# A new order of loads, masks and first outputs in the start-up of a fused attention and gated feed-forward kernel

## The chip, the cores and the metric

The kernel runs on one core of a Trainium2 chip. The metric is the device time of one execution in microseconds (us). The profile covers a "span" that is about 2.1 us shorter than that time, and all moments below are counted from the start of the span. PE is the matrix engine, PEld its weight loads, DVE the vector engine, ACT the scalar engine, POOL the engine that issues the casting loads. In these traces each engine works through its instructions in the order in which the program gives them, so an instruction that waits holds up everything behind it on its engine (in the changed kernel a scaled q on DVE, ready since about 11.6, starts at 13.38, behind a product that could start only at 12.77); this is what the whole case turns on.

## The reference, cut to what matters

```python
def reference(q, k, v, lam, w_gate, w_val, w_out):      # q, k, v: 4 x 8 x 768 x 64
    # block-wise linear attention with a decay lam per head
    for each block of the sequence:
        intra = (q_b @ k_b.T * decay_mask) @ v_b
        inter = (q_b * lam**(i+1)) @ kv_state
        attn  = intra + inter
        kv_state = lam**block * kv_state + (k_b * lam**(block-1-i)).T @ v_b
    x = attn as 3072 x 512
    return (sigmoid(x @ w_gate) * (x @ w_val)) @ w_out    # 512 -> 1536 -> 512
```

The kernel uses blocks of 128 rows, six of them, each with the four batches b0 to b3. In block 0 there is no state yet, so it needs: transposes of q and k on PE, scaled q (`QS`, DVE), copies of k (`KS`, ACT), scores (`sp`, PE), masked products (`MT`, DVE: scores times mask), the attention output (`op`, PE, from `MT` and v), its copy (`XT`, ACT), and then gate and value products of the feed-forward part, tile by tile.

## The kernel before

The helpers that matter, in the order of the data. Cuts are marked with `# ...`.

```python
    load(0, "k", 0, 2)          # k of b0 and b1 in one load; all these are issued by POOL and cast to bf16
    load(0, "k", 2, 4)
    load(0, "q", 2, 3)          # q of b0, b1 come uncast over two other queues (q0f, q1f)
    load(0, "q", 3, 4)
    load(0, "v", 0, 1)          # then v1, v2, gate weights, value weights, v3, more weights
    # ...
    def idle(n):                # products on zeros, only to keep PE busy
        for i in range(n):
            nc.tensor.matmul(wm, lhsT=zero[:, :C], rhs=zero, start=True, stop=True, skip_group_check=True)

    def piece_tq0(bs, then=None):
        tq = ps_at.tile([128, 2, 2, 2 * C], BF16, name="tq", tag="ps")
        for b in bs:            # four PE transposes of q per batch
            # ...
                transpose_pair(tq[:, b % 2, g // 2, g % 2 * C:g % 2 * C + C], Q[0], b, g)
        if then:
            then()
        for b in bs:            # DVE: scaled q
            nc.vector.tensor_tensor(out=QS[0, b // 2][...], in0=tq[:, b % 2], in1=lamq0_e, op=ALU.mult)

    def piece_s(n, bs, pool=ps_at, tag="ps"):   # PE: 8 score products per batch, needs KS and QS
    def piece_m(n, b, us=(0, 1)):               # DVE: two masked products per batch, needs sp
    def piece_a0(b, split=()):                  # PE: output of batch b, needs MT and v; then XT copy on ACT

    idle(10)
    nc.vector.tensor_copy(Q[0][:, 0], q01[0])   # cast of q of b0
    piece_tq0([0])
    make_mask(0)
    idle(1)
    piece_tq0([1])
    piece_tk0(0)                                # k transposes of b0 and b1, and their copies on ACT
    make_mask(1)
    idle(1)
    piece_s(0, [0])
    piece_m(0, 0)
    piece_s(0, [1])
    piece_m(0, 1, (0,))
    piece_tk0(1)
    nc.scalar.preload_act_table_set("sigmoid_and_others")
    piece_tq0([2])
    piece_tq0([3])
    piece_m(0, 1, (1,))
    piece_s(0, [2], ps_ff, "ff")
    piece_m(0, 2)
    piece_s(0, [3])
    piece_m(0, 3)
    make_kd0(0, nc.vector)
    piece_a0(0)
    piece_a0(1)
    idle(2)
    piece_a0(2, (nc.scalar.copy, nc.scalar.copy))
    g0 = psum()
    mm_part(g0, WG, 0, 0, 0, 3 * C)             # gate of tile 0 for b0 to b2
    v0 = psum()
    mm_part(v0, WV, 0, 0, 0, 3 * C)
    piece_a0(3, (nc.scalar.copy, nc.vector.tensor_copy))
    # ... gate and value of tiles 1 to 8
    t(1, 0)                                     # block 1: q transposes, scaled q, k transposes, one k copy on ACT
    gv(0, 9)                                    # gate and value of tile 9
    sc(1, 0)                                    # scores of block 1
    # ...
```

## Time and profile before

| | before |
|---|---|
| time, median of 6 runs | 226.62 us (226.21 to 226.88) |
| span of the profiled run | 224.5 us |
| PE at full speed from | 6.02 us, to the end |
| first scores / first gate product / output of b3 on PE | 8.65 / 14.51 / 15.90 us |

From the page of the kernel before: the span, the busy time of PE, and two rows of the 40 slices (5.6 us each): the busy tenths of PE and the clock that it was granted. The clock row shows 9 in its first slice too, though PE ran at half speed until 6.02 (its idle products start 0.43 us apart there, those at 12.97 only 0.23): time before the first recorded step of the clock is not seen in the row, nor in a run's mean clock (1.0 for this profiled run).

```profile
span 224.5 us, 4262 instructions
...
PE 217.8 (97%) x1746; PEld 114.7 (51%) x1746; DVE 105.8 (47%) x192; ACT 79.8 (36%) x151; POOL 79.2 (35%) x78
...
PE   7689999999999999999999999999999999999994
...
PEclk9999999999999999999999999999999999999999
```

PE is full from the fourth slice on. A new order can only win in the first three slices (16.8 us) or in small holes later.

The start-up on PE and on DVE, from the timeline of the kernel before. The columns are start, duration, engine, line, operation, out<-in, shape and count; the bracket says how long the engine had been idle and who released it.

```profile
8.65 0.89 PE L300 MATMUL sp<-QS,KS 64*128 64x128 bf16 x16 [0.24 <-ACT KS L267]
...
11.66 0.73 PE L300 MATMUL sp<-QS,KS 64*128 64x128 bf16 x16 [0.29 <-DVE QS L256]
12.31 0.72 PE L313 MATMUL op<-MT,vb 128*64 128x128 bf16 x16
12.97 0.60 PE L153 MATMUL wm<-zero 128*128 128x512 bf16 x2
13.51 0.65 PE L313 MATMUL op<-MT,vb 128*64 128x128 bf16 x8
14.51 0.81 PE L434 MATMUL gp<-XT,WG 128*128 128x384 bf16 x4 [0.35 <-ACT XT L352]
15.15 0.81 PE L434 MATMUL gp<-XT,WV 128*128 128x384 bf16 x4
15.90 0.41 PE L313 MATMUL op<-MT,vb 128*64 128x128 bf16 x8
```

```profile
9.08 1.89 DVE L202 TENSOR_TENSOR MT<-sp,mask 128x512 bf16<-128x512 f32 x3 [0.73 <-PE sp L300]
11.18 0.76 DVE L256 TENSOR_TENSOR QS<-tq,lamq 128x512 bf16<-128x512 bf16 x2 [0.21 <-PE tq L238]
11.85 3.07 DVE L202 TENSOR_TENSOR MT<-sp,mask 128x512 bf16<-128x512 f32 x5
```

When v of b3 lands is read from the timeline of POOL (first line below: the issue) and the view of loads for that issue (second line: the time to landing is the last number).

```profile
9.56 0.94 POOL L91 DMA_DIRECT2D vb<-in_v_dram  x1
...
vb<-in_v_dram POOLq DMA_DIRECT2D x1, 128.0 KB, 6.2
```

So it lands at about 9.56 + 6.2 = 15.76, and PE uses it at 15.90. In the same way the first gate weights land at 14.2 and the first value weights at 14.9.

In block 1 (timeline of PE) the k transposes take longer than the q transposes, 8 products each:

```profile
31.45 0.61 PE L281 MATMUL tq<-ident,qb 128*128 128x128 bf16 x8
31.90 0.78 PE L281 MATMUL tk<-ident,kb 128*128 128x128 bf16 x8
...
34.90 1.04 PE L420 MATMUL gp<-XT,WG 128*128 128x512 bf16 x4
```

### The profile page before, as it was taken

To read this page: it belongs to the slowest core of one execution; us is meant where nothing else is said; L and a number is where in the kernel's file an instruction comes from. 1 tells how busy PE (TensorE), PEld (TensorE's weight loads), DVE (VectorE), ACT (ScalarE), POOL (GpSimd) and SP (SyncE) were. 2 spreads that over 40 slices of the span, in tenths; PEclk is the share of its full clock that TensorE was granted. 3 is DMA by queue.
4 is the path that set the end of the run, shared out by engine and by line. 5 is a ranking of instruction groups with operands and counts; after the bars stand their busy time and mean duration, and the time that the engine had idled before them with its cause. 6 is when DMAs were issued, how large, how long until landed. Compare 5 with 4: busy or idle time off the path is not lost.

```text
span 224.5 us, 4262 instructions
## 1 busy us (share of the span) xinstructions
PE 217.8 (97%) x1746; PEld 114.7 (51%) x1746; DVE 105.8 (47%) x192; ACT 79.8 (36%) x151; POOL 79.2 (35%) x78
## 2 busy tenths in 40 slices
PE   7689999999999999999999999999999999999994
PEld 2454455888854454444445444446444445444443
DVE  7797747595521713336732445742335840333300
ACT  5564334435422234333225333115333225333221
POOL 8996698983592008930006940000000000000000
PEclk9999999999999999999999999999999999999999
DMA  6999999999999992999021999021930012100022
GB/s 109 155 169 193 191 176 155 163 183 168 157 162 159 225 236 86 210 157 101 1 96 55 231 151 128 0 96 47 168 70 0 0 52 91 47 3 0 0 93 95
DMA packets 106419, 25.70 MB, mean 114 GB/s; under 512 B 97056, under 2 KB 103456, under 8 KB 106400
## 3 DMA queue, kind: packets, MB, share of 16 engines
q0 software_dynamic: 81792, 13.90, 81.6%
q1 hardware_dynamic: 23568, 11.28, 20.4%
q10 hardware_dynamic: 1040, 0.26, 0.5%
q8 instruction: 13, 0.21, 0.4%
q14 instruction: 6, 0.05, 0.1%
HBM read 28.32 MB, written 6.29 MB: 154 GB/s over the span
## 4 chain that ended last, share of the span: by engine, by line
PE 94%; DMA 3%; ACT 1%; issue 1%; DVE 0%; POOLq 0%
PE po L483 27%; PE gp L420 21%; PE vp L426 21%; PE gp L455 5%; PE gp L434 5%; PE vp L461 5%; PE sp L300 3%; PE op L313 3%; DMA kb<-in_k_dram 3%; PE op L325 1%; PE po L472 1%; PE cp L404 1%; ACT KS L267 1%; PE tk L238 1%; ACT XT L352 0%
## 5 line engine op out<-in xcount | busy, mean ns | idle before, releaser
L429 DVE TENSOR_TENSOR ht<-sg,vp 128x512 bf16<-128x512 bf16 x54 | 37.1, 687 | 64.2 <-PE vp L426 64.0
L483 PE MATMUL po<-WO,ht 128*128 128x512 bf16 x276 | 62.0, 379 | 0.0
L420 PE MATMUL gp<-XT,WG 128*128 128x512 bf16 x216 | 55.5, 379 | 0.0
L426 PE MATMUL vp<-XT,WV 128*128 128x512 bf16 x216 | 55.4, 379 | 0.0
L423 ACT ACTIVATE sg<-gp 128x512 bf16<-128x512 f32 x54 | 32.2, 597 | 59.0 <-PE gp L420 59.0
L483 PEld LDWEIGHTS <-ht 128*128 128x128 bf16 x276 | 26.3, 98 | 31.0
L426 PEld LDWEIGHTS <-WV 128*128 128x128 bf16 x216 | 21.2, 98 | 25.5
L420 PEld LDWEIGHTS <-WG 128*128 128x128 bf16 x216 | 20.8, 98 | 24.7
L486 ACT COPY ob<-po 128x512 f32<-128x512 f32 x23 | 13.5, 586 | 52.2 <-PE po L483 50.4
L204 DVE TENSOR_TENSOR MT<-sp,mask 128x512 bf16<-128x512 f32 x40 | 25.1, 682 | 9.1 <-PE sp L300 9.1
L382 POOL TENSOR_TENSOR sd<-Sb,dec 128x512 f32<-128x512 bf16 x8 | 8.1, 1037 | 41.2 <-DVE Sb L411 41.1
L455 PE MATMUL gp<-XT,WG 128*128 128x256 bf16 x96 | 14.4, 273 | 0.0
L461 PE MATMUL vp<-XT,WV 128*128 128x256 bf16 x96 | 14.4, 273 | 0.0
L465 DVE TENSOR_TENSOR ht<-sg,vp 128x256 bf16<-128x256 bf16 x24 | 10.0, 420 | 8.6 <-PE vp L461 8.6
L458 ACT ACTIVATE sg<-gp 128x256 bf16<-128x256 f32 x24 | 9.2, 384 | 13.0 <-PE gp L455 11.8
L91 POOL DMA_DIRECT2D vb<-in_v_dram x10 | 12.7, 1278 | 1.0 <-DMA WG<-in_moe_w_gate_dram 0.6
L373 POOL TENSOR_TENSOR kd<-kb,kds 128x1024 bf16<-128x1024 bf16 x6 | 11.3, 1904 | 4.7 <-PE vp L461 4.7
L411 DVE TENSOR_TENSOR Sb<-cp,sd 128x512 bf16<-128x512 f32 x8 | 5.2, 686 | 15.5 <-PE cp L404 15.5
L340 ACT CAST XT<-op 128x512 bf16<-128x512 f32 x19 | 9.9, 598 | 2.1 <-PE op L313 2.0
L455 PEld LDWEIGHTS <-WG 128*128 128x128 bf16 x96 | 9.2, 98 | 1.7 <-issue 0.2
L461 PEld LDWEIGHTS <-WV 128*128 128x128 bf16 x96 | 9.4, 98 | 1.1
L77 POOL DMA_DIRECT2D qb<-in_q_dram x8 | 9.4, 1182 | 0.0
(79 smaller groups left out, 162.1 us busy)
## 6 DMA issues: line engine op xcount, KB each, us to landing
out_dram<-ob SPq DMA_DIRECT2D x21, 256.0 KB, 2.0
kb<-in_k_dram POOLq DMA_DIRECT2D x10, 256.0 KB, 8.4
qb<-in_q_dram POOLq DMA_DIRECT2D x8, 256.0 KB, 8.1
vb<-in_v_dram POOLq DMA_DIRECT2D x4, 512.0 KB, 13.7
WO<-in_moe_w_out_dram POOLq DMA_DIRECT2D x3, 512.0 KB, 8.7
WV<-in_moe_w_val_dram POOLq DMA_DIRECT2D x5, 256.0 KB, 8.8
WG<-in_moe_w_gate_dram POOLq DMA_DIRECT2D x4, 256.0 KB, 8.6
qb<-in_q_dram POOLq DMA_DIRECT2D x6, 128.0 KB, 8.3
```

What stands on the lines that cost most here:

```text
L91: nc.gpsimd.dma_start(out=lst[n][:, b0:b1], in_=src[b0:b1, :, sl, :].rearrange("b h s d -> s (b h) d"))
L204: nc.vector.tensor_tensor(out=out.rearrange("p (e x) c -> p e x c", e=2), in0=x.rearrange("p (e x) c -> p e x c", e=2), in1=mask.rearrange ...
L373: nc.gpsimd.tensor_tensor(out=KD[n][:, e], in0=K[n][:, e], in1=kds[:, e::2].unsqueeze(1).unsqueeze(3).to_broadcast([128, B, HP, D]), op=AL ...
L420: nc.tensor.matmul(gp, lhsT=WG[:, mt, fs], rhs=x[:, mt, :], start=(mt == 0), stop=(mt == NMT - 1))
L423: nc.scalar.activation(sg, gp, AF.Sigmoid)
L426: nc.tensor.matmul(vp, lhsT=WV[:, mt, fs], rhs=x[:, mt, :], start=(mt == 0), stop=(mt == NMT - 1))
L429: nc.vector.tensor_mul(HT[n, ft], sg, vp)
L434: nc.tensor.matmul(ps[:, lo:hi], lhsT=W[:, mt, ft * 128:(ft + 1) * 128], rhs=x[:, mt, lo:hi], start=(mt == 0), stop=(mt == NMT - 1))
L455: nc.tensor.matmul(gp[:, cs], lhsT=WG[:, mt, fs], rhs=x[:, mt, cs], start=(mt == 0), stop=(mt == NMT - 1))
L461: nc.tensor.matmul(vp[:, cs], lhsT=WV[:, mt, fs], rhs=x[:, mt, cs], start=(mt == 0), stop=(mt == NMT - 1))
L483: nc.tensor.matmul(po, lhsT=HT[n, ft][:, tt * 128:(tt + 1) * 128], rhs=WO[:, ft, :], start=(ft == 0), stop=(ft == NFT - 1))
L486: nc.scalar.copy(ob, po)
```

## The change

It wants to start the chain of block 0 earlier and to take waits out of PE: k of b0 gets its own load; both masks are made before the scaled q of b1; the k transposes of b2 and b3 come together before their copies; the output of b0 goes between the scores of b2 and b3, with the scaled q of b3 queued behind the first masked product of b2; fewer idle products before the first real work (ten become five, and two become one further down), which now start after the count on DVE; and in block 1 the gate of tile 9 stands between the q and k transposes, while the k copy is shared by ACT and DVE. Core of the diff:

```diff
-    nc.vector.memset(zero, 0.0)
     # ... count ip1
+    nc.vector.memset(zero, 0.0)
-    load(0, "k", 0, 2)
+    load(0, "k", 0, 1)
+    load(0, "k", 1, 2)
-    idle(10)
+    idle(5)
     nc.vector.tensor_copy(Q[0][:, 0], q01[0])
     piece_tq0([0])
     make_mask(0)
+    make_mask(1)
     idle(1)
     piece_tq0([1])
     piece_tk0(0)
-    make_mask(1)
+    piece_tk0(1)
     idle(1)
     piece_s(0, [0])
     piece_m(0, 0)
     piece_s(0, [1])
-    piece_m(0, 1, (0,))
-    piece_tk0(1)
+    piece_m(0, 1)
+    piece_tk0(2, 3)
     nc.scalar.preload_act_table_set("sigmoid_and_others")
     piece_tq0([2])
-    piece_tq0([3])
-    piece_m(0, 1, (1,))
-    piece_s(0, [2], ps_ff, "ff")
-    piece_m(0, 2)
+    def first():
+        piece_s(0, [2], ps_ff, "ff")
+        piece_m(0, 2, (0,))
+    piece_tq0([3], first)      # transposes of b3, then first(), then the scaled q of b3
+    piece_m(0, 2, (1,))
+    piece_a0(0)
     piece_s(0, [3])
     piece_m(0, 3)
     make_kd0(0, nc.vector)
-    piece_a0(0)
     piece_a0(1)
-    idle(2)
+    idle(1)
 # ... block 1
-    t(1, 0)
-    gv(0, 9)
+    scale(1, 0, turn(Q))
+    g9 = psum()
+    mm_part(g9, WG, 0, 9, 0, TCH)
+    sigm(0, 9, g9)
+    tk = turn(K)
+    KS[1, 0] = trsb.tile([128, 2, 2, 2, C], BF16, tag="KS", name="KS")
+    nc.scalar.copy(KS[1, 0][:, 0], tk[:, 0])
+    nc.vector.tensor_copy(KS[1, 0][:, 1], tk[:, 1])
+    v9 = psum()
+    mm_part(v9, WV, 0, 9, 0, TCH)
+    prod(0, 9, v9)
```

More of the change, by code (lines that the diff above doesn't have):

```diff
@@ L257, in piece_tq0, with piece_tk0 @@
                                     in0=tq[:, b % 2], in1=lamq0_e, op=ALU.mult)
-    def piece_tk0(bp):
-        KS[0, bp] = trsb.tile([128, 2, 2, 2, C], BF16, tag="KS", name="KS")
-        for i in range(2):
-            if i == 0 or bp == 0:
-                tk = ps_at.tile([128, 1 + bp, 2, 2 * C], BF16, name="tk", tag="ps")
-            x = tk[:, i if bp else 0]
+    def piece_tk0(*bs):
+        bp = bs[0] // 2
+        if (0, bp) not in KS:
+            KS[0, bp] = trsb.tile([128, 2, 2, 2, C], BF16, tag="KS", name="KS")
+        tk = ps_at.tile([128, len(bs), 2, 2 * C], BF16, name="tk", tag="ps")
+        for j, b in enumerate(bs):
@@ L265, in piece_tk0 @@
             for g in range(HP):
-                transpose_pair(x[:, g // 2, g % 2 * C:g % 2 * C + C], K[0], 2 * bp + i, g)
-            nc.scalar.copy(KS[0, bp][:, :, i].rearrange("p e x c -> p e (x c)"), x)
+                transpose_pair(tk[:, j, g // 2, g % 2 * C:g % 2 * C + C], K[0], b, g)
+        for j, b in enumerate(bs):
+            nc.scalar.copy(KS[0, bp][:, :, b % 2].rearrange("p e x c -> p e (x c)"), tk[:, j])
     def piece_t(n, bp):
-        if n > 1 or bp == 1:
-            scale(n, bp, QR[n][:, :, 2 * bp:2 * bp + 2] if n > 1 else HB["q"])
-            return
@@ L273, in piece_t @@
-        q1, k1 = (x[1][:, 0].rearrange("p (e b y d) -> p e b y d", e=2, b=2, y=HP) for x in (Q, K))
-        tq = ps_at.tile([128, 2, 2, 2, C], BF16, name="tq", tag="ps")
-        tk = ps_at.tile([128, 2, 2, 2, C], BF16, name="tk", tag="ps")
-        def turn(out, x):
-            for e in range(2):
-                for i in range(2):
-                    for g in range(2):
-                        nc.tensor.transpose(out[:, e, i, g, :],
-                                            x[:, e, i, 2 * g:2 * g + 2, :].rearrange("p y d -> p (y d)"), ident)
@@ L284, in piece_t, with turn @@
-        turn(tq, q1)
-        scale(n, bp, tq)
-        turn(tk, k1)
-        KS[n, bp] = trsb.tile([128, 2, 2, 2, C], BF16, tag="KS", name="KS")
-        nc.scalar.copy(KS[n, bp], tk)
+        scale(n, bp, QR[n][:, :, 2 * bp:2 * bp + 2] if n > 1 else HB["q"])
+    def turn(x):
+        x = x[1][:, 0].rearrange("p (e b y d) -> p e b y d", e=2, b=2, y=HP)
+        out = ps_at.tile([128, 2, 2, 2, C], BF16, name="tq", tag="ps")
+        for e in range(2):
+            for i in range(2):
+                for g in range(2):
+                    nc.tensor.transpose(out[:, e, i, g, :],
+                                        x[:, e, i, 2 * g:2 * g + 2, :].rearrange("p y d -> p (y d)"), ident)
+        return out
```

## The prediction

> What bounds the kernel now. The page gives PE 97% busy over a 224.5 us span; after the third slice PE shows 9 everywhere. So only the first 16.7 us can be shortened, plus small holes later. All edits lie before 37 us.
>
> The ramp (timeline, chain of waits). k of b0 and b1 lands at 7.53; KS copies on ACT from 8.01 (0.59 each); first score product 8.65; then DVE is nearly solid from 9.08 to 16.05 (masked products 0.61 apart). After 12.3, though, loads matter. From the issue and landing views: v2 lands near 13.5, the first gate weights 14.2, value weights 14.93, v3 15.76. Against these PE starts the output of b2 at 13.50, the gate at 14.51, value at 15.15, output of b3 at 15.90. However early the masked products are, the output of b3 can gain at most 0.13 us. Load order and bytes do not change, and the queue moves at a constant rate from 5.5 us (about 77 KB of bf16 per 0.5 us), so v3 should not land earlier; splitting k costs POOL one more issue (0.9 us for 128 KB, 1.16 for 256 KB: about +0.65), which the queue's backlog hides.
>
> What the change does there, my estimates. k0 lands near 6.8 instead of 7.53; first score product 8.1 (was 8.65); first masked product 8.5 (9.08). Both k transposes of b2, b3 now precede their copies, which removes the 0.67 us PE wait on ACT at 10.53. Last masked product ends near 14.6 (14.9). The second mask (0.68) ahead of the second scaled q is harmless. Moving the zero fill (0.22) fills a hole in the DVE start-up, but the cast of q0 still waits for q0's landing at about 4.94. Most of this ends in waits for weights and v3: gain kept 0.1 us.
>
> Later loads. Value weights for tile 4 land at 23.5, used at 23.68, so no more than 0.18 us may be gained before that. In block 1 the second half of k lands at 32.28; PE's k transposes stop there for 0.163 us (32.066 to 32.285, where 0.056 is normal). The change puts the gate of tile 9 (0.86 us) between the q and k transposes, so that wait goes, and ACT's 1.01 us k copy is split between ACT and DVE, just ready for the scores. Gain 0.16, and the earlier 0.1 passes through. Sum: about 0.27 us. The next load (value weights, 35.2, used at 35.77) leaves it room.
>
> Risk. The clock record goes to full at 6.02 us; idle products before are 0.427 apart (half speed). [...] Idle products now start near 3.1 and last 2.1 us[...]. Slack before v3 hides a late clock up to about 12[...].
>
> Predicted 226.35 us (226.66 before), range 225.9 to 226.8. Chances: faster by over 2% 0.005, within 2% 0.985, slower 0.01.
>
> Right if: v3's output on PE still starts at 15.75 to 15.9; PE waits longer for v3 or weights; the 0.16 us hole in block 1's k transposes is gone; PE from 40 us on is the same trace shifted by 0.2 to 0.35. Wrong if: full clock comes after 10 us; v3 and weights land over 0.15 us earlier or later (POOL late, or the queue starting earlier); k copies now hold up block 1's scores at about 34.1.

The sum came to about 0.27 us faster, 0.1 kept in the start-up and 0.16 in block 1. The "about 12" is the author's estimate, set against the landings of v2 (13.5), weights (14.2, 14.93) and v3 (15.76).

## More of the kernel before

The scores of b2 and b3 come in one group at 11.66, both scaled q having been made together at 11.18. DVE is then never idle from 11.18 to 16.05. The outputs of b0 and b1 follow at once.

## The result, and the profile after

The change is slower: median 229.19 us of six runs, against 226.62. The ratio is 1.0103, with a 95% interval of 1.007 to 1.0137: a loss of 1%, clear of the noise, though within the 2% to which the prediction gave a chance of 0.985. Ratios here are the mean time of one kernel's fast runs over that of the other's fast runs of the same rounds, so not quite the ratio of the medians. The six runs are not one cloud. They are 227.95 and 227.99 with a mean granted clock of 1.0; 229.16, 229.22 and 229.23 with 0.991 or 0.992; and 230.0 with 0.993. All count as fast runs: the slowest is 0.9% above the fastest.

The same rows of the page of the changed kernel:

```profile
span 227.1 us, 4230 instructions
...
PE 216.9 (95%) x1717; PEld 115.8 (51%) x1740; DVE 105.0 (46%) x193; ACT 79.4 (35%) x151; POOL 80.0 (35%) x79
...
PE   4969999999999999999999999999999999999994
...
PEclk9978999999999999999999999999999999999999
```

The clock row has a 7 and an 8 in the third and fourth slice (its first two 9s are again before the first recorded step). The record of clock steps in the two traces has the detail (0.5 is half speed):

```
before   full speed from 6.02 to the end
changed  full 11.34 to 14.75, half 14.75 to 18.17, full from 18.17 to the end
```

PE of the changed kernel reached full speed 5.3 us later, and lost it again for one stretch of 3.41 us. The timelines of PE and DVE of the changed kernel over the same work:

```profile
8.84 1.04 PE L294 MATMUL sp<-QS,KS 64*128 64x128 bf16 x16
...
12.35 0.40 PE L294 MATMUL sp<-QS,KS 64*128 64x128 bf16 x8 [0.76 <-DVE QS L257]
12.68 0.41 PE L307 MATMUL op<-MT,vb 128*64 128x128 bf16 x8
13.94 0.40 PE L294 MATMUL sp<-QS,KS 64*128 64x128 bf16 x8 [0.84 <-ACT XT L346]
14.27 0.41 PE L307 MATMUL op<-MT,vb 128*64 128x128 bf16 x8
15.04 0.64 PE L307 MATMUL op<-MT,vb 128*64 128x128 bf16 x8 [0.37 <-issue]
15.94 1.44 PE L428 MATMUL gp<-XT,WG 128*128 128x384 bf16 x4 [0.25 <-ACT XT L346]
17.17 1.31 PE L428 MATMUL gp<-XT,WV 128*128 128x384 bf16 x4
18.41 0.41 PE L307 MATMUL op<-MT,vb 128*64 128x128 bf16 x8
```

```profile
9.48 2.48 DVE L203 TENSOR_TENSOR MT<-sp,mask 128x512 bf16<-128x512 f32 x4 [1.05 <-PE sp L294]
11.88 0.41 DVE L257 TENSOR_TENSOR QS<-tq,lamq 128x512 bf16<-128x512 bf16 x1
12.77 0.69 DVE L203 TENSOR_TENSOR MT<-sp,mask 128x512 bf16<-128x512 f32 x1 [0.47 <-PE sp L294]
13.38 0.41 DVE L257 TENSOR_TENSOR QS<-tq,lamq 128x512 bf16<-128x512 bf16 x1
13.71 1.94 DVE L203 TENSOR_TENSOR MT<-sp,mask 128x512 bf16<-128x512 f32 x3
```

Read the two together. DVE makes the scaled q of b2 at 11.88, and PE can then do the scores of b2 (12.35). The next thing in DVE's order is the first masked product of b2, which waits 0.47 us for those scores. Only behind it, at 13.38, comes the scaled q of b3, whose transposes had been done since about 11.6. So the scores of b3 start at 13.94 (11.98 before, by the single records), and the output of b1, which stands behind them in PE's order although nothing it needs is missing, at 14.27 (12.62 before). The release of the scores at 13.94 is put down to ACT, but the scaled q that they read ended at 13.38 + 0.41 = 13.79, so DVE is the more likely one. The trace of e1, an experiment below with the same order, puts the same wait down to DVE:

```profile
13.24 0.40 PE L294 MATMUL sp<-QS,KS 64*128 64x128 bf16 x8 [0.84 <-DVE QS L257]
```

Gate and value of tile 0 start at 15.94 and then run at half speed: the gate's 4 products take 1.23 us to the start of the value's, where they took 0.65.

| moment on PE, us | before | changed | later by |
|---|---|---|---|
| scores of b2 | 11.66 | 12.35 | 0.69 |
| scores of b3 | 11.98 | 13.94 | 1.96 |
| gate of tile 0 | 14.51 | 15.94 | 1.43 |
| output of b3 | 15.90 | 18.41 | 2.51 |
| first q transpose of block 1 | 31.45 | 33.97 | 2.51 |
| gate of tile 10 | 34.90 | 37.51 | 2.61 |
| span | 224.5 | 227.1 | 2.6 |

With the old warm-up (e1) the scores of b2 start at 11.66, as before, and those of b3 at 13.24: the 0.69 goes with the late warm-up, and 1.26 of the 1.96 with the order.

So 1.43 us are lost before the gate of tile 0, 1.08 between it and the output of b3 (half speed), 0.10 in block 1, and nothing after. The loads had no part in it: v of b3 was issued at 10.24 and landed 5.6 us later (both from the same views), at about 15.84, 0.1 later than before.

```profile
10.24 0.95 POOL L91 DMA_DIRECT2D vb<-in_v_dram  x1
...
vb<-in_v_dram POOLq DMA_DIRECT2D x1, 128.0 KB, 5.6
```

Block 1 of the changed kernel, from the timeline. The DVE half of the k copy begins only when the ACT half is over, and the scores stretch to 0.89 us because their second half waits for it (0.62 before):

```profile
35.97 0.58 ACT L605 COPY KS<-tq 128x512 bf16<-128x512 bf16 x1
36.58 0.42 DVE L606 COPY KS<-tq 128x512 bf16<-128x512 bf16 x1 [1.06 <-ACT KS L605]
...
36.68 0.89 PE L294 MATMUL sp<-QS,KS 64*128 64x128 bf16 x16
```

### The profile page after: what moved, and what is told of

The parts are those of the page before. It is cut to its first block, busy times and chain, and to the rows that moved or that the text cites. A ratio compares the mean times of both kernels' runs of the same rounds, so it can differ in the third digit from the quotient of the medians.

```text
span 227.1 us, 4230 instructions
## 1 busy us (share of the span) xinstructions
PE 216.9 (95%) x1717; PEld 115.8 (51%) x1740; DVE 105.0 (46%) x193; ACT 79.4 (35%) x151; POOL 80.0 (35%) x79
## 4 chain that ended last, share of the span: by engine, by line
PE 92%; ACT 2%; DMA 2%; issue 1%; DVE 0%; SPq 0%
PE po L477 26%; PE gp L414 20%; PE vp L420 20%; PE gp L428 6%; PE gp L449 5%; PE vp L455 5%; PE sp L294 3%; PE op L307 3%; DMA q1f<-in_q_dram 2%; PE op L319 1%; PE po L466 1%; PE cp L398 1%; PE tk L239 1%; ACT XT L346 1%; ACT L508 1%
## 5 line engine op out<-in xcount | busy, mean ns | idle before, releaser
L423 DVE TENSOR_TENSOR ht<-sg,vp 128x512 bf16<-128x512 bf16 x53 | 36.4, 687 | 62.7 <-PE vp L420 58.4
L477 PE MATMUL po<-WO,ht 128*128 128x512 bf16 x266 | 61.3, 379 | 0.5
L414 PE MATMUL gp<-XT,WG 128*128 128x512 bf16 x207 | 54.0, 379 | 0.4
L420 PE MATMUL vp<-XT,WV 128*128 128x512 bf16 x208 | 53.5, 379 | 0.1
L417 ACT ACTIVATE sg<-gp 128x512 bf16<-128x512 f32 x53 | 31.6, 597 | 59.3 <-PE gp L414 58.2
L480 ACT COPY ob<-po 128x512 f32<-128x512 f32 x23 | 13.5, 586 | 52.2 <-PE po L477 48.4
L449 PE MATMUL gp<-XT,WG 128*128 128x256 bf16 x96 | 14.4, 273 | 0.0
L455 PE MATMUL vp<-XT,WV 128*128 128x256 bf16 x96 | 14.4, 273 | 0.0
```

The lines of the kernel that those rows point to most:

```text
L414: nc.tensor.matmul(gp, lhsT=WG[:, mt, fs], rhs=x[:, mt, :], start=(mt == 0), stop=(mt == NMT - 1))
L417: nc.scalar.activation(sg, gp, AF.Sigmoid)
L420: nc.tensor.matmul(vp, lhsT=WV[:, mt, fs], rhs=x[:, mt, :], start=(mt == 0), stop=(mt == NMT - 1))
L423: nc.vector.tensor_mul(HT[n, ft], sg, vp)
L449: nc.tensor.matmul(gp[:, cs], lhsT=WG[:, mt, fs], rhs=x[:, mt, cs], start=(mt == 0), stop=(mt == NMT - 1))
L455: nc.tensor.matmul(vp[:, cs], lhsT=WV[:, mt, fs], rhs=x[:, mt, cs], start=(mt == 0), stop=(mt == NMT - 1))
```

## The experiments

All ratios are to the kernel before. For the change that is the six runs above; for the experiments its runs had medians of 226.63 to 226.71 and lay between 226.19 and 227.24 (44 runs); their clock was never under 0.998. "Falls" counts runs whose mean clock was 0.993 or lower. One stretch of 3.41 us at half speed lowers the mean by 0.0075 over such a span, to 0.992, two to 0.985 (profiled: 0.991 in the changed kernel with one, 0.985 in e6 with two).

| run | what it is | median us (range) | ratio | falls | profile: gate of tile 0 |
|---|---|---|---|---|---|
| changed | the change | 229.19 (227.95 to 230.0) | 1.0103 | 4 of 6 | 15.94 |
| e1 | change, old warm-up | 227.92 (227.28 to 230.42) | 1.0071 | 3 of 6 | 15.35 |
| e2 | before, new warm-up | 226.56 (226.46 to 227.97) | 1.0000 | 0 of 6 | 14.66 |
| e3 | change, seven idle products | 228.46 (227.26 to 229.58) | 1.0069 | 4 of 6 | 15.75 |
| e4 | e1, one k copy | 228.53 (227.35 to 229.73) | 1.0077 | 4 of 6 | 15.53 |
| e5 | change, old order from q of b3 on | 227.19 (227.08 to 227.86) | 1.0022 | 0 of 6 | 14.96 |
| e6 | before, new order only | 227.28 (227.17 to 229.76) | 1.0040 | 1 of 6 | 16.32 |
| e7 | e1, the hole filled | 227.55 (227.39 to 228.08) | 1.0036 | 0 of 6 | 15.47 |
| e8 | before, block 1 with two k tiles | 227.01 (one run 1272.96) | 1.0009 | (outlier) | none |
| e9 | e1, one line moved | 227.6 (226.8 to 227.81) | 1.0028 | 0 of 6 | 14.42 |
| e10 | before, k split only | 227.45 (226.46 to 228.19) | 1.0023 | 1 of 6 | 14.57 |
| e11 | e8 again | 227.43 (226.63 to 227.84) | 1.0025 | 0 of 6 | 14.56 |
| e12 | before, block 1 as changed | 227.2 (226.68 to 227.42) | 1.0018 | 0 of 6 | 14.60 |
| e13 | e11, two PSUM tiles | 226.94 (226.25 to 227.2) | 1.0004 | 0 of 6 | 14.95 |
| e14 | change, one line moved | 227.27 (227.03 to 227.62) | 1.0026 | 0 of 6 | 15.45 |
| e15 | useful parts together | 226.91 (226.18 to 227.2) | 1.0005 | 1 of 6 | 14.72 |

### Is it the warm-up? e1, e2, e3

The first theory was the obvious one from the clock record: fewer and later idle products bring the full clock late. Its rival was the new order. e1 undoes the warm-up in the change:

```diff
+    nc.vector.memset(zero, 0.0)      # first again, not after the count
-    idle(5)
+    idle(10)
```

> The change, with only its warm-up undone: zero fill first again and ten idle products. Clock theory (the loss is the late full clock and its fall back to half): full clock at about 6 us in the record and no fall back, gate of tile 0 at full speed (0.162 us apart), time 226.3 to 226.9. Rival (the new order of the ramp itself costs, by making the scores of b3 wait for the scaled q and outputs): still 227.5 or more with a full clock.

Measured: the profile reached full speed at 7.11, and fell back at 13.93 for one stretch of 3.42 us all the same. Three of six runs fell. The theory had said no falls, and it was wrong there. The runs fall into levels that can be read off: 227.28, 227.30 and 227.33 without a fall, 228.51 with one, 229.68 and 230.42 with two. One fall costs 228.51 - 227.30 = 1.2 us. The level without a fall is 0.6 above before.

e2 puts only the new warm-up into the kernel before:

```diff
-    nc.vector.memset(zero, 0.0)      # moved after the count
-    idle(10)
+    idle(5)
```

> The kernel before, with only the new warm-up: zero fill after the count, five idle products. Clock theory: full clock not before 9 us, time 227.5 to 229.5, spread of runs over 1 us. Rival (order): 226.4 to 226.9, as before.

Measured: full speed at 8.09 instead of 6.02, and no loss: five of six runs at 226.46 to 226.73, one, unexplained, at 227.97 with a clock of 1.0. The theory had asked for 227.5 or more. So in the old order full speed at 8.09 is harmless; at 11.34, as in the change, it was not tried by itself.

e3 is the change with `idle(7)` for `idle(5)`:

> The change with seven idle products instead of five, still starting near 3.0 us (they then end near 6.0, past the first q transposes' earliest start of 5.75). Clock theory: [...] full clock comes by 6 to 9 us in most runs, time 226.6 to 227.6, below the change's. Rival: the same 228 to 229 as the change.

Measured: full speed at 6.38, as hoped, and still 228.46, with four falls. So the first theory falls: the change loses its clock again whatever the warm-up was. The warm-up adds something in the new order: without falls the change runs at 227.97, e1 at 227.30.

e4 is e1 with one k copy on ACT in block 1:

```diff
-    nc.scalar.copy(KS[1, 0][:, 0], tk[:, 0])
-    nc.vector.tensor_copy(KS[1, 0][:, 1], tk[:, 1])
+    nc.scalar.copy(KS[1, 0], tk)
```

> As e1, and the k copy of block 1 again one ACT copy. In the profile of the change the DVE half of that copy waited for the ACT half (36.58, right after 35.97+0.58), and PE's scores waited 0.25 us for it. Theory (split into one tile runs one after the other and costs): the hole in the scores changes, from 35.28 (end of k transposes) one copy of 1.01 us after the sigmoid would end near the same time, so within 0.1 us of e1. Rival (the split does help, without it PE waits longer): 0.1 to 0.3 slower than e1.

Measured: levels of 227.35, 228.5 and 229.7, the same as e1 within 0.1 us: in the time the split gave nothing. In the trace the stretch from the first q transpose of block 1 to the gate of tile 10 is 3.62 us, against 3.54 in e1, so the split gains 0.08 there.

### The new order: e5, e6, e14, e9

e5 is the change with the order from the scaled q of b3 on as before (warm-up, k split, masks and block 1 stay changed):

```diff
     piece_tq0([2])
-    def first(): ...
-    piece_tq0([3], first)
-    piece_m(0, 2, (1,))
-    piece_a0(0)
+    piece_tq0([3])
+    piece_s(0, [2], ps_ff, "ff")
+    piece_m(0, 2)
     piece_s(0, [3])
     piece_m(0, 3)
     make_kd0(0, nc.vector)
+    piece_a0(0)
     piece_a0(1)
-    idle(1)
+    idle(2)
```

> The change with only its order from the scaled q of b3 on undone: scores of b2 and b3, then all masked products, then the outputs of b0 and b1; five idle products and the late zero fill stay. Order theory (the scaled q of b3 stands on DVE behind the first masked product of b2, which waits for PE, so the scores of b3 and the output of b1 behind them come 1.2 us late, and PE is then so thin that the clock falls to half for one window): no fall back of the clock in any run, gate of tile 0 at 14.3 to 14.7, time 226.4 to 226.9 with a spread under 1 us. Rival (warm-up with the k split or the masks is the cause): 227.3 or more, with fall backs.

Measured: no falls, gate of tile 0 at 14.96, 227.19. The falls went, as the theory said; the time is 0.3 above its range. Full speed came at 11.68 in that profile, and a part of the late warm-up probably shows: e10, with the same k split and as late a q but full speed from 6.38, had that gate at 14.57. The late clock was not tried alone.

e6 is the reverse, the kernel before with the new order alone (the diff's lines from `piece_m(0, 1)` to `piece_a0(1)`, keeping its own `piece_tk0(1)` and `idle(2)`):

> The kernel before with only that new order; ten idle products, zero fill first, and the two idle products before the output of b2 kept. Order theory: scores of b3 after 13.0 (11.98 before), gate of tile 0 at 15.2 to 15.6, levels of 227.2 (clock 1.0) and about 1.2 more for each window that falls to half. Rival: 226.4 to 226.9, no falls.

Measured: five runs at 227.17 to 227.53 with a clock of 1.0, and the profiled one at 229.76 with two stretches of 3.41 us at half speed (13.11 to 19.93). The scores of b3 came at 13.35 in its profile; the gate, at 16.32, is later than expected because that execution had the falls. So the order alone costs about 0.6 us without any fall, and it can bring falls into a kernel that never had one in 44 runs.

Which part of the order? The theory points at one line: the scaled q of b3. e14 is the whole change, with that alone moved ahead:

```diff
-    piece_tq0([3], first)
+    piece_tq0([3])
+    first()
```

> The change with only the line of the scaled q of b3 moved ahead of the scores and masked product of b2 (e9 without the old warm-up). Theory: no falls of the clock in any run; levels near 227.1 (late full clock, as e5) and 227.8 (with the late load of value weights that e9 and e10 showed), so median 227.1 to 227.8 against 229.2 of the change. Rival (late warm-up and split matter more than that line): 228 or more, with falls.

Measured: 227.27, no falls. Of the change's ratio of 1.0103, 1.0026 is left. The profiled run had a late q load (its cast began at 5.91 instead of 5.27), so its late gate is no measure.

e9 is the same line with the old warm-up:

> As e1 (the change with the old warm-up), with one line moved: the scaled q of b3 goes to DVE before the scores and first masked product of b2; the output of b0 still stands between the scores of b2 and b3. Theory (the scaled q behind that masked product is what delays the scores of b3 and what stands behind them): scores of b3 at 12.3 to 12.6 (13.24 in e1), gate of tile 0 at 14.4 to 14.8 (15.35), no falls of the clock, 226.6 to 227.0. Rival (the output of b0 between the scores is the cost): still about 227.3, with falls.

The timeline of DVE in e9 shows both scaled q together again, and the four masked products of b2 and b3 without a wait:

```profile
11.24 0.74 DVE L257 TENSOR_TENSOR QS<-tq,lamq 128x512 bf16<-128x512 bf16 x2
12.12 2.48 DVE L203 TENSOR_TENSOR MT<-sp,mask 128x512 bf16<-128x512 f32 x4
```

Scores of b3 at 12.38, gate of tile 0 at 14.42, as expected, no falls. The output of b0 still stands between the scores, so that is not the cost. The time had two levels, 226.8 (two runs) and 227.6 to 227.8 (four runs), so its median of 227.6 lies above the expected range. The profile is of the upper level: PE waits 0.71 us there for value weights, and e10 has that wait without this line.

### Why the clock falls: e7

The falls might come from PE having too little to do around 12 to 14 us. e7 keeps the new order and the old warm-up and fills the hole with idle products:

```diff
     piece_a0(0)
+    idle(4)
     piece_s(0, [3])
     # ...
-    idle(1)
+    idle(2)
```

> As e1 (change with the old warm-up), with four idle products in the hole before the scores of b3 (0.86 us at full speed) and two instead of one before the output of b2. Theory: the falls come from PE being thin there, so none or few now; the order cost stays: 227.2 to 227.5 in nearly all runs. Rival (falls come from elsewhere[...]): 227.3, 228.5 and 229.7 as often as in e1.

Measured: no fall in six runs (three of six in e1), 227.39 to 228.08: the order's cost stays and the falls go. The view of stretches, over 3.41 us that end where the clock changed in e1 and in the changed kernel, and at the same spacing in e7 and before, in that order (columns: stretch, its length, PE busy, count, and the view's other columns):

```profile
10.52:13.93 3.41, 1.94 (x40) 1.00 2.24 162
```

```profile
11.34:14.75 3.41, 1.74 (x36) 1.00 2.15 165
```

```profile
11.60:15.01 3.41, 3.11 (x47) 1.00 2.14 166
```

```profile
6.02:9.43 3.41, 2.41 (x34) 1.00 2.45 156
9.43:12.85 3.42, 2.45 (x52) 1.00 2.39 156
```

After 1.94 (e1) and 1.74 us (changed) of work in such a stretch the clock fell; after 2.41 and 2.45 (before) and 3.11 (e7) it stayed. In all five profiles with a fall (changed, e1, e3, e4, e6) PE had been busy for 1.57 to 1.94 us of the last 3.41, so 46 to 57%: it was thin, not idle, and its longest pause there in the changed kernel was 1.06 us (from one start to the next). In the eleven readable profiles without a fall, the lightest stretch looked at after full speed had 1.95 us (e11). The two ranges all but touch, and some matmul records are missing from these traces, so no limit is read from them. Transposes are counted in these figures. Alone they take 1.23 of the 2.45 us in the second stretch of the kernel before, which kept the clock, and 0.51 of the 1.94 in e1's, which lost it; without them the two would stand the other way round (1.30 against 1.43; records of the two kinds overlap).

The steps of the changed kernel's clock are 3.41 us apart (11.34, 14.75, 18.17). Full speed first came anywhere from 4.5 (e11) to 11.7 us (e5) in these profiles. In the changed kernel PE was busy for 2.77 us of 4.51 to 7.93, and for all of 7.93 to 11.34, at whose end full speed came. By what rule the clock is stepped, these runs do not show.

### The k split: e10

```diff
-    load(0, "k", 0, 2)
+    load(0, "k", 0, 1)
+    load(0, "k", 1, 2)
```

> The kernel before with only k of b0 and b1 in two loads. In the profile of the change q of b0 and b1 landed 0.3 us later (cast of q0 at 5.27 against 4.95, of q1 at 6.35 against 6.01). Theory: the two loads of k reach the queue earlier[...], so here too q0 and q1 land 0.2 to 0.4 later and k of b0 lands near 6.8; the k transposes still come after those of q1, at 7.3 to 7.5 (7.57 before); time 226.5 to 226.9, no gain. Rival (the q loads are late for another reason): casts at 4.95 and 6.01, k transposes at 7.0, 226.4.

Measured: k transposes at 7.34 instead of 7.57, gate of tile 0 at 14.57, so no gain there; casts of q at 5.35 and 6.43. Late q loads were also seen without the split (casts at 5.22 in e12, 5.56 in e13, 5.46 in e15) and early ones only without it: four of the seven readable profiles without the split had the cast before 5.0, none of the nine with it. That speaks for the split, but whether it delays q is not settled. The time has levels again, 226.46 and 226.66, then 227.45 three times, and one run with two falls (228.19). So a fall is not peculiar to the new order. The profiled run, at the upper level, shows the reason, in the timeline of PE: the value weights of tile 1 were awaited for 0.73 us.

```profile
19.04 0.82 PE L435 MATMUL gp<-XT,WV 128*128 128x512 bf16 x3 [0.73 <-DMA WV<-in_moe_w_val_dram]
```

That load took 7.1 us to land, after 5.5 for the one before it. In all sixteen readable traces one packet of 16384 bytes of the kind "instruction" took about 0.9 us, beginning between 16.8 and 17.7 (before: 0.95 from 16.84; changed: 0.89 from 16.96). In fifteen of them a weight load of about that time took 0.4 to 1.6 us more than the one before it; in e7 it took 0.1 more. In the kernel before this was the next load (landing at 18.9, used at 19.36), which hides it; in e9 and e10 it was the one that PE waits for. That the packet causes the delay is argued from the moments, not tested.

### Block 1: e8, e11, e12, e13

e8 puts block 1's change into the kernel before, with the two halves of k in two tiles (shown against the change):

```diff
-    KS[1, 0] = trsb.tile([128, 2, 2, 2, C], BF16, tag="KS", name="KS")
-    nc.scalar.copy(KS[1, 0][:, 0], tk[:, 0])
-    nc.vector.tensor_copy(KS[1, 0][:, 1], tk[:, 1])
+    k10 = [trsb.tile([128, 2, 2, C], BF16, tag=f"KS1{e}", name=f"KS1{e}", bufs=1) for e in range(2)]
+    KS[1, 0] = k10
+    nc.vector.tensor_copy(k10[1], tk[:, 1])
+    nc.scalar.copy(k10[0], tk[:, 0])
```

> The kernel before with only the change of block 1 (gate of tile 9 between the q and k transposes, k copy split), but the two halves of k in two tiles, DVE's half not waiting for ACT's. Theory: the split into one tile is what held up the scores, so here no hole before or within the scores: from the first q transpose of block 1 to the gate of tile 10 3.28 us (3.44 before, 3.54 in the change), time 0.1 to 0.2 under before. Rival (ACT's half, behind the sigmoid, ends too late anyway): 3.4 or more, no gain.

Its profiled execution took 1272.96 us: PE did its 512-column products 1.28 us apart (the median, from beginning to end), six times the usual 0.216, while DVE and ACT took their usual times. That trace has no clock record, so that it was the clock is not shown. The run is counted as slow and says nothing about the edit; its other runs were 226.69 to 227.53. e11 is the same kernel again, and e12 has block 1 exactly as in the change:

> e8 again, whose profiled run was an outlier of 1273 us with PE six times slower throughout, so that its trace says nothing. Theory: 3.28 us from the first q transpose of block 1 to the gate of tile 10 (3.44 before, 3.54 in the change), time 0.1 to 0.2 under before, perhaps lost in the spread. Rival: 3.4 or more.

> The kernel before with the change of block 1 exactly as in the change (both halves of the k copy into one tile). Theory: 3.54 us for that stretch, 0.1 over before and 0.26 over e11 in the trace; DVE's half starts as ACT's ends. Rival (the stretch is late in the change only because PE comes there at another time): 3.3.

Measured, from first q transpose to the gate of tile 10: e12 3.54 us, as in the change and 0.10 over before; e11 3.61, not 3.28. In e11 ACT's half began at 33.92, just after DVE's half, so two destination tiles did not separate the halves. What they still shared was the source, one PSUM tile of 2 KB per partition. In this trace DVE's half ended at 33.47 + 0.42 = 33.89, and ACT's began at 33.92, put down to DVE's, though ACT had been free for 0.31 us:

```profile
33.92 0.59 ACT L605 COPY KS<-tq 128x512 bf16<-128x512 bf16 x1 [0.31 <-DVE KS L604]
```

The times of e11 and e12 are 0.8 and 0.5 us over the kernel before, more than the stretch explains; the rest is open. Whether the shared PSUM tile orders the halves is what e13 tests. It gives each half its own PSUM tile:

```diff
+        out = [ps_at.tile([128, 2, 2, C], BF16, name="tq", tag="ps") for e in range(2)]
-    nc.vector.tensor_copy(k10[1], tk[:, 1])
-    nc.scalar.copy(k10[0], tk[:, 0])
+    nc.vector.tensor_copy(k10[1], tk[1])
+    nc.scalar.copy(k10[0], tk[0])
```

> As e11 (kernel before with block 1's gate between the transposes and the k copy in two tiles), and the two halves of k also in two PSUM tiles. Theory (the shared PSUM tile orders the halves): ACT's half starts right after the sigmoid, about 33.6, not after DVE's; scores at 34.2 or earlier; 3.28 us from first q transpose to the gate of tile 10 (3.44 before, 3.50 in e11). Rival (something else orders them): as e11.

The timeline of e13 has the halves side by side, and the scores without a hole:

```profile
33.86 0.42 DVE L614 COPY KS<-tq 128x512 bf16<-128x512 bf16 x1 [0.40 <-PE tq L291]
33.91 0.58 ACT L615 COPY KS<-tq 128x512 bf16<-128x512 bf16 x1
34.62 0.62 PE L305 MATMUL sp<-QS,KS 64*128 64x128 bf16 x16
```

The stretch is 3.27 us, 0.17 less than before. But e2, e6 and e10 leave block 1 as it was and take 3.27 too: PE came to it at 31.60 or later, not at 31.45, and did not have to wait for k. So 3.27 is the stretch without that wait. Two PSUM tiles take the wait out and add none; one tile adds 0.27. In the time (1.0004) the 0.17 is not seen: the runs of either kernel are spread over a microsecond.

### Can the useful parts win? e15

e15 is the change with k in one load, the old warm-up, the moved line of e14 and block 1 of e13.

> The change with k of b0 and b1 in one load again, the old warm-up, the scaled q of b3 ahead of the scores of b2, and block 1 as in e13. Theory: the ramp is bound by v3 and the weights as before, so the gate of tile 0 at 14.3 to 14.6 and output of b3 at 15.9; 0.16 gained in block 1: 226.4 to 226.6, at most 0.2 under before, and inside its spread. Rival (there was something to gain in the ramp): under 226.2.

Measured: 226.91, ratio 1.0005 (0.9987 to 1.0023); gate of tile 0 at 14.72, output of b3 at 16.12, block 1 3.27. It lies above its expected range and does not beat the kernel before. One of its six runs had a clock of 0.992, so its start-up is not safe from falls either.

## Why the prediction was wrong

The sum was 0.27 us faster, and the measured median is 2.6 slower, outside the range. Point by point:

- *"v3 should not land earlier", "the queue's backlog hides" POOL's extra issue, k of b0 "near 6.8".* Right: v3 at 15.84, k of b0 at 1.26 + 5.5 = 6.76.
- *"First score product 8.1", "first masked product 8.5".* They came at 8.84 and 9.48, later than before (8.65 and 9.08), although k of b0 landed 0.75 us earlier. Its transposes stand on PE behind the q transposes of b1 (7.02), and those behind the cast of q1 (6.35). So the earlier k gave little: 8.36 in e1 with the old warm-up, 8.41 in e10.
- *"Last masked product ends near 14.6"; "Most of this ends in waits for weights and v3: gain kept 0.1 us."* This is the step that failed. It ended at 13.71 + 1.94 = 15.65 in the change, and at 14.95 in e1. I had laid DVE's instructions end to end and had not followed who waits for whom: the first masked product of b2 waits for PE, the scaled q of b3 is behind it on DVE, the scores of b3 wait for that, and the output of b1 is behind those on PE. PE was at the gate at 15.94, well after its weights (about 14.4), so the bound by loads that capped the gain never came into play. Moving that one line back (e14) takes the change from 229.19 to 227.27.
- *"Slack before v3 hides a late clock up to about 12."* In the old order full speed at 8.09 cost nothing (e2), though at 11.68 something may show (e5). In the new one there was no slack left, and the late clock costs 227.97 - 227.30 = 0.67 us (change against e1, runs without a fall).
- *The risk named was a late full clock.* The larger one, losing it again because the new order thins PE, was not thought of. It costs about 1.2 us per stretch at half speed (e1: 228.51 - 227.30), struck four of six runs, and went when the hole was filled (e7) or the line moved (e9, e14). Single runs of e10 and e15 had falls too, so other orders are not wholly safe.
- *"Gain 0.16" in block 1, the split copy "just ready for the scores".* The wait for k did go, but the halves of the copy share one PSUM tile and ran one after the other (ACT's to 36.55, DVE's from 36.58): 0.10 lost instead, and the scores stretched by 0.27. With two PSUM tiles the stretch is 0.17 shorter (e13), but it is as short in the old order whenever PE comes 0.15 us later (e2).
- *"the cast of q0 still waits for q0's landing at about 4.94."* It began at 5.27; q's landing varies between runs by 0.6 us even without the k split, and whether the split adds to it stays open.

Two of the conditions that the prediction itself had named as "wrong if" held: full speed came after 10 us (11.34), and the k copies held up block 1's scores.

Put together from the levels, a run of the change with one fall is 226.6 before + 0.6 (order and the rest of the edits, e1 without a fall) + 0.7 (late clock) + 1.2 (one fall) = 229.1.

## What to carry to other kernels

When an instruction is moved on one engine, walk both in-order queues: ask what stands behind it, what that releases on the other engine, and what stands behind that there. In a start-up, idle products belong in the holes as much as before the first work: here the clock fell after 3.41 us with 1.57 to 1.94 us of work on PE (five profiles), and four idle products in the hole took the falls from three of six runs (e1) to none of six (e7). To share one copy between two engines, give each its own PSUM tile: with two the halves ran side by side (e13, from 33.86 and 33.91), with one in turn (e11, from 33.47 and 33.92).
